# Chunk 1's second projection as seven products of quarters, four more blocks transposed by DMA, and new order tables

## The chip, the core and the metric

The kernel runs on one core of a Trainium2 chip. The metric is the device time of one execution in microseconds (us), the median over runs. The engines are named as in the profile: PE (TensorE matmul), PEld (its weight loads), DVE (VectorE), ACT (ScalarE), POOL (GpSimd), SP (SyncE, which here only issues DMAs).

## The reference, cut to what matters

A linear attention with decay over 64-token blocks gives an array x of 3072 tokens by 512; two projections with a sine between them follow.

```python
def _attn_ref(q, k, v, lam):            # (4, 8, 768, 64) each, lam (8,)
    ...
    for b in range(nb):
        ...
        intra = np.einsum('bhic,bhjc->bhij', qb, kb) * Dmask[None]
        intra = np.einsum('bhij,bhjd->bhid', intra, vb)
        inter = np.einsum('bhid,bhde->bhie', qb * lam_pow[None], kv_state)
        out[:, :, sl] = intra + inter
        kv_state = lam_block[None, :, None, None] * kv_state + np.einsum('bhsd,bhse->bhde', kb_dec, vb)

def _moe_ref(x, w_in, w_out, alpha):    # (3072, 512), (512, 2048), (2048, 512), (2048,)
    h = x @ w_in
    s = np.sin(alpha * h)
    g = h + s * s / (alpha + 1e-09)
    return (g @ w_out).astype(np.float32)
```

## The kernel before, in words

**Blocks and chunks.** The attention is done in 24 blocks of 128 tokens, 6 for each of the 4 batches. Four blocks make a chunk of 512 tokens, and there are 6 chunks, 0 to 5. Chunk 0 is blocks 0 to 3, and so on. While PE works on the projections of one chunk, the attention of later blocks is put between its matmuls.

**Attention of a block.** `load_q` and `load_kv` bring q, k and v as float32 through SP's queue (rings of six blocks). `scale_block` writes them as bfloat16: q and k are multiplied by powers of lam (`L462`, `L472`, `L480`, `L492`), v is only copied (`L486`, `L495`). Then q and k have to be transposed into `qkT`. For blocks under `TD` = 12 PE does it (`piece_Q` for q of two blocks, `L534`; `piece_T` for k of one, `L511`; `piece_K` in the first blocks), and DVE or ACT copy the result out of PSUM (`L516`, `L543`). For blocks from `TD` on SP issues one DMA that transposes both (`L501`). `piece_G(s, t)` is the rest on PE: the scores of block s (`L612`), whose product with the mask is DVE's `Sm` (`L623`), and the output (`L694`, `L707`, `L716`) and the state (`L656`) of block t. The output goes to `xT` (`L726`), the state to `Zd` or `Zc` (`L666`, `L672`).

**First projection.** `unit_A` (`L822`, four matmuls of 512 columns) or `unit_A2` (`L856`, eight of 256) makes one 128-row slice of h, or two halves of slices, in one PSUM bank. ACT takes the sine (`L832`, `L866`), ACT or POOL squares it (`L836`/`L837`, `L870`/`L871`), DVE adds (`L839`, `L874`) and writes `gT`. Three banks take turns.

**Second projection, plain.** In chunks under `SC` = 2, that is 0 and 1, `unit_B` adds up 16 slices for 128 tokens in four steps of four matmuls of 512 columns (`L887`): 64 matmuls for a chunk. ACT copies each of the four results (`L901`) and a DMA stores it.

**Second projection by seven products.** From chunk `SC` on the product of `gT` and `w2` is cut into quarters, and seven products of quarters take the place of eight. `weight_sums` (`L930`) makes five sums or differences of quarters of `w2`, three in buffers of their own and two in place over `w2`; `token_sums` (`L953`) makes five of `gT` for each chunk, in four parts each, 20 instructions for a chunk. `unit_P` (`L975`) is one product for 128 tokens, eight matmuls of 256 columns; 14 of them make a chunk. `finish` takes each result out of PSUM: products 3 and 1 by a copy (`L1012`), the others by an add or a subtraction on DVE (`L1015`, `L1021`).

**Order.** The program first lists its steps with what each reads and writes, and numbers them. Tables written out by hand in `_Plan.ORDER` say for PE, ACT, DVE, POOL and SP in which order the engine takes the steps; where a step is allowed on several engines, the table in which it stands decides. Every engine works through its list strictly in order, and semaphore waits are derived from reads and writes. A pair such as `(42,112)` in PE's table is filler: 42 matmuls of 112 columns on a constant tile (`L1134`), whose result nobody reads.

**Beside it.** `weight_sums(True)` stands ahead of chunk 2's units and `weight_sums(False)`, the two in place, ahead of chunk 3's. A key "select" in reads and writes keeps POOL's `affine_select` steps at the start apart.

Of the kernel before, what the change touches and what calls it, by code (L numbers as in the profile page):

```python
# [13 lines left out]
class _Op:  # L14


    def __init__(self, eng, emit, dur, reads, writes, dma, after, issue, lat, runs=64):
# [13 lines left out]
        self.knows = None  # L31


class _Plan:
# [17 lines left out]
        ),  # L52
        "ACT": (
# [16 lines left out]
        ),  # L70
        "DVE": (
# [30 lines left out]
        ),  # L102
    }

# [104 lines left out]
def bass_lightning_attn__then__act_snake_kernel(  # L209
# [15 lines left out]
    NB = S // BL  # L225
# [1020 lines left out]
```

## Time and profile before

| What | Value |
|---|---|
| Times of three runs | 210.68, 211.11, 211.37 us; median 211.11 us |
| Profiled execution | span 209.8 us from the first to the last instruction; the page gives no other time for it |
| Busy share of the span | PE 97%, PEld 64%, DVE 76%, ACT 76%, POOL 60% |
| Granted TensorE clock | 1.000 of full speed, mean over the span |
| HBM read, written | 27.28 MB, 6.29 MB |
| Chain that ended last, by engine | PE 83%, DVE 6%, DMA 3%, SP's queue 3%, ACT 2% |

The three runs lie 0.9 to 1.6 us above the span of the profiled execution: an execution's time also holds what lies around its first and last instruction. A busy share is an average over the whole span. A matmul's end is modelled in the trace, so what PE needs for a group is better read from the chain of waits, which gives a group's time on the path, than from the durations of its matmuls. Rows of the view of groups give busy time and the mean of one instruction, then the idle time of the engine ahead of it.

### The profile page before, as it was taken

The numbers are of one execution on the slowest core, as the hardware profiler recorded it, in microseconds if no ns is written. First come the engines' busy times: TensorE is split into PE (matmuls) and PEld (weight loads), VectorE is DVE, ScalarE is ACT, GpSimd is POOL, SyncE is SP. The second block draws the span as 40 slices with busy tenths as digits, with TensorE's granted clock in tenths as the row PEclk, the third lists the DMA queues.
The fourth block names the chain that finished last, engine by engine and source line by source line (L and its number), as shares of the span: only waits on it lengthen the run. The fifth ranks groups of instructions, "written<-read, shape, count | busy, mean of one in ns | idle before, by whom it ended". The sixth has DMA issues, their size and how long they took to land.

```text
span 209.8 us, 4867 instructions
## 1 busy us (share of the span) xinstructions
PE 203.5 (97%) x1975; PEld 134.3 (64%) x1975; DVE 160.3 (76%) x266; ACT 158.7 (76%) x294; POOL 126.9 (60%) x130
## 2 busy tenths in 40 slices
PE   7979999999999999999998999999999999999995
PEld 6847444457677776555555667766667765666894
DVE  4884557563999866868899799889698699777643
ACT  4949995968998989999997887787963889568210
POOL 7075354994469578679885392944581957378300
DMA  4999999999998999999999920190000004000514
GB/s 141 310 318 232 206 213 237 246 229 256 220 264 205 227 245 230 223 233 196 246 271 228 213 53 0 33 271 2 3 0 3 0 23 179 3 0 0 200 40 163
DMA packets 78998, 33.35 MB, mean 159 GB/s; under 512 B 55408, under 2 KB 76160, under 8 KB 78976
## 3 DMA queue, kind: packets, MB, share of 16 engines
q1 hardware_dynamic: 73744, 27.14, 56.2%
q0 software_dynamic: 3696, 3.67, 10.5%
q10 hardware_dynamic: 1536, 2.24, 3.3%
q8 instruction: 15, 0.25, 0.5%
q14 instruction: 7, 0.06, 0.1%
HBM read 27.28 MB, written 6.29 MB: 160 GB/s over the span
## 4 chain that ended last, share of the span: by engine, by line
PE 83%; DVE 6%; DMA 3%; SPq 3%; ACT 2%; issue 1%
PE bank L822 27%; PE bank L975 22%; PE bank L887 13%; PE bank L856 10%; DMA v<-in_v_dram 3%; PE bank L716 3%; SPq L315 3%; PE bank L612 3%; DVE gT L839 2%; PE bank L694 1%; DVE Sm L623 1%; PE bank L511 1%; PE bank L656 1%; DVE w L930 1%; PE bank L534 1%; PE bank L707 1%
## 5 line engine op out<-in xcount | busy, mean ns | idle before, releaser
L822 PE MATMUL bank<-xT,w 128*128 128x512 bf16 x296 | 70.5, 379 | 0.0
L839 DVE SCALAR_TENSOR_TENSOR gT<-u,rinv,bank 128x512 bf16<-128x512 bf16 x74 | 53.6, 742 | 18.2 <-ACT u L836 12.5
L832 ACT ACTIVATE t<-bank,alpha 128x512 bf16<-128x512 f32 x74 | 50.0, 684 | 21.0 <-PE bank L822 20.5
L822 PEld LDWEIGHTS bank<-xT,w 128*128 128x128 bf16 x296 | 28.3, 98 | 28.4 <-DVE gT L839 0.4
L836 ACT ACTIVATE u<-t 128x512 bf16<-128x512 bf16 x59 | 36.5, 628 | 1.3
L837 POOL TENSOR_TENSOR u<-t 128x512 bf16<-128x512 bf16 x15 | 16.0, 1066 | 34.1 <-ACT t L832 30.5
L953 POOL TENSOR_TENSOR gT<-gT 128x512 bf16<-128x512 bf16 x24 | 27.8, 1172 | 11.2 <-DVE Xs L953 6.0
L623 DVE TENSOR_TENSOR Sm<-bank,mask 128x1024 bf16<-128x1024 f32 x24 | 29.1, 1218 | 4.3 <-PE bank L648 1.8
L887 PE MATMUL bank<-w,gT 128*128 128x512 bf16 x128 | 31.4, 380 | 0.0
L874 DVE SCALAR_TENSOR_TENSOR gT<-u,rinv,bank 128x256 bf16<-128x256 bf16 x44 | 18.8, 476 | 7.8 <-ACT u L870 6.1
L472 POOL TENSOR_TENSOR qk<-q,Lq 128x512 bf16<-128x512 f32 x20 | 21.2, 1075 | 2.8 <-DMA q<-in_q_dram 2.8
L856 PE MATMUL bank<-xT,w 128*128 128x256 bf16 x176 | 22.2, 273 | 0.0
L492 POOL TENSOR_TENSOR qk<-k,Lk 128x512 bf16<-128x512 f32 x20 | 20.9, 1053 | 0.6 <-DMA k<-in_k_dram 0.6
L866 ACT ACTIVATE t<-bank,alpha 128x256 bf16<-128x256 f32 x44 | 18.9, 476 | 2.0 <-PE bank L856 1.5
L887 PEld LDWEIGHTS bank<-w,gT 128*128 128x128 bf16 x128 | 11.7, 98 | 12.2
L856 PEld LDWEIGHTS bank<-xT,w 128*128 128x128 bf16 x176 | 16.4, 98 | 3.5 <-issue 0.3
L953 POOL TENSOR_TENSOR Xs<-gT 128x512 bf16<-128x512 bf16 x13 | 16.1, 1235 | 1.5 <-DVE gT L839 1.4
L975 PE MATMUL bank<-w,gT 128*128 128x256 bf16 (+1 forms) x136 | 16.3, 266 | 0.0
L975 PE MATMUL bank<-w,Xs 128*128 128x256 bf16 (+1 forms) x136 | 16.0, 267 | 0.1
L975 PE MATMUL bank<-ws,gT 128*128 128x256 bf16 x128 | 15.8, 273 | 0.0
L975 PEld LDWEIGHTS bank<-w,gT 128*128 128x128 bf16 x136 | 12.6, 98 | 3.2
L975 PEld LDWEIGHTS bank<-w,Xs 128*128 128x128 bf16 x136 | 12.4, 98 | 2.8 <-DVE osb L1021 0.3
(101 smaller groups left out, 276.0 us busy)
## 6 DMA issues: line engine op xcount, KB each, us to landing
q<-in_q_dram SPq DMA_DIRECT2D x12, 512.0 KB, 6.2
k<-in_k_dram SPq DMA_DIRECT2D x24, 256.0 KB, 5.5
v<-in_v_dram SPq DMA_DIRECT2D x24, 256.0 KB, 5.4
out_dram<-osb SPq DMA_DIRECT2D x14, 256.0 KB, 2.5
w<-in_moe_w_out_dram POOLq DMA_DIRECT2D x4, 512.0 KB, 11.4
w<-in_moe_w_in_dram POOLq DMA_DIRECT2D x3, 512.0 KB, 9.0
ws<-in_moe_w_in_dram SPq DMA_DIRECT2D x2, 512.0 KB, 7.5
out_dram<-osb ACTq DMA_DIRECT2D x8, 128.0 KB, 4.0
```

What stands on the lines that cost most here:

```text
L472: lambda e, a=a: e.tensor_tensor(qk2[:, j:j + 2, 4 * a:4 * a + 4, :], q32[:, jq, 4 * a:4 * a + 4, :, :].rearrange("p h t d -> p t h d"), b ...
L492: lambda e: e.tensor_tensor(qk2[:, j, H:2 * H, :], block32(k32, jl), lk, ALU.mult), 1.05,
L623: op("DVE", lambda e: e.tensor_tensor(Sm[js][:, :, :], banks[:, 512 * b0:512 * b0 + 1024].rearrange("p (c i) -> p c i", i=128), bass.AP(ma ...
L822: ins = e.matmul(ps[hb][:, c0:c1], w1[:, kc, 128 * m:128 * (m + 1)], xT[x][:, kc, c0:c1], start=(kc == 0 and c0 == lo), stop=(kc == NKC - ...
L832: op("ACT", lambda e: e.activation(t16[ju][:, w], ps[hb][:, w], ACTF.Sin, scale=alpha[:, m:m + 1]), 0.69 if hi - lo == TCH else 0.475, [ba ...
L836: lambda e: (e.activation(u16[ju][:, w], t16[ju][:, w], ACTF.Square) if e is nc.scalar else e.tensor_tensor(u16[ju][:, w], t16[ju][:, w], ...
L839: op("DVE", lambda e: e.scalar_tensor_tensor(out=gT[g][:, m, w], in0=u16[ju][:, w], scalar=rinv[:, m:m + 1], in1=ps[hb][:, w], op0=ALU.mul ...
L856: ins = e.matmul(ps[hb][:, 256 * i:256 * i + 256], w1[:, kc, 128 * (m + i):128 * (m + i + 1)], xT[x][:, kc, lo:lo + 256], start=(kc == 0 a ...
L866: op("ACT", lambda e, i=i: e.activation(t16[ju][:, 256 * i:256 * i + 256], ps[hb][:, 256 * i:256 * i + 256], ACTF.Sin, scale=alpha[:, m + ...
L887: ins = e.matmul(ps[ob][:, w], gT[g][:, m, 128 * s4:128 * (s4 + 1)], w2[:, m, w], start=(m == 0), stop=(m == NM - 1),)
L953: e.tensor_tensor(dst, in0, in1, alu), 0, rd, wr))
L975: ins = e.matmul(ps[ob][:, lo + d0:lo + d1], lhs, rhs[:, d0:d1], start=first and p == 0, stop=(p == NM // 2 - 1), skip_group_check=True)
```

## The change

It does six things at once.

1. `SC` becomes 1. Chunk 1's second projection is done by seven products: 14 `unit_P` in place of 16 steps of `unit_B`, with 20 `token_sums` instructions more. Both calls of `weight_sums` move ahead of the second halves of chunk 1's first projection. From chunk 2 on `piece_G` takes its output bank from the three banks of the first projection (before from chunk 3 on).
2. `TD` becomes 8. Blocks 8 to 11 are transposed by DMA. Their `piece_Q` (two) and `piece_T` (four) on PE go, and with them the copies out of PSUM. What followed from `TD` before as the first block of a loop follows from a new constant, `LB` = 12.
3. Most copies and scalings may stand on several engines: `AD` is ACT or DVE, `DP` is DVE or POOL, `ADP` all three.
4. "select" goes. Where a POOL step is marked `some` (four of the `affine_select`), it and its neighbours on POOL wait for one another through a semaphore.
5. Four activations at the start (`Lq4`, `Lp`, `Lk`, `Lq`) also read `warm`, so they stand behind the table load of the exponential.
6. All five order tables are new.

What the new tables say, counted step by step (before, then after):

| Kind of step | before | after |
|---|---|---|
| copies of v | ACT 20, POOL 4 | ACT 4, POOL 15, DVE 5 |
| scalings of q and k | DVE 7, POOL 41 | DVE 15, POOL 33 |
| `token_sums` | DVE 43, POOL 37 | DVE 50, POOL 50 |
| `weight_sums` | DVE 7, POOL 3 | DVE 5, POOL 5 |
| results of products out of PSUM | DVE 28, ACT 10 | DVE 38, ACT 7 |
| results of `unit_B` out of PSUM | ACT 8 | ACT 2, DVE 2 |
| copies of transposes out of PSUM | DVE 9, ACT 11 | DVE 6, ACT 8 |
| DMA transposes on SP | 12 | 16 |

From the second halves of chunk 1's first projection on, PE's table has the products of chunk 1 between chunk 2's units where the steps of `unit_B` stood. SP's table has the loads up to q of block 10, then the transposes of blocks 8 and 9, then v of 8 and 9, the transposes of 10 and 11, v of 10; before, v of blocks 8 and 9 stood ahead of q of block 10. POOL's table has, from q of block 4 to the last scaling that the transpose of block 8 reads: two q of block 4, a square, k of 4, a weight sum, v of 4, a weight sum, one q of 6, a weight sum, k of 7, k of 8, a square, two q of 8. At the start the fillers are (15,128), (15,512), then (12,128) and (7,128); before they were 102 in 10 groups, the first (42,112) and (30,128). ACT issues its DMA for alpha behind the first logarithm, not ahead of it, and `Lq4` is the last of the four exponentials, not the first. Two of the four first scalings of q and two of the four of k are POOL's; before one of eight was.

The diff, with the tables left out:

```diff
+        self.some = False
+        self.strict = None
...
-        if d.eng != o.eng or d.dma is not None:
+        if d.eng != o.eng or d.dma is not None or d is o.strict:
...
+        last = None
+        for o in order:
+            if o.eng == "POOL" and o.dma is None:
+                if last is not None and (o.some or last.some):
+                    o.strict = last
+                    o.deps.add(last)
+                last = o
...
-    TD = 12
+    TD = 8
+    LB = 12
...
-    SC = 2
-    QD = ((0, 0), (0, 2), (1, 0), (1, 2))
+    SC = 1
+    AD = (("ACT", 0, 0), ("DVE", 0, 0))
+    DP = (("DVE", 0, 0), ("POOL", 0, 0))
+    ADP = (("ACT", 0, 0), ("DVE", 0, 0), ("POOL", 0, 0))
...
-                   ported(op(QE(a, t),
+                   ported(op(DP,
...
-                ported(op((("ACT", 0.62, 0.0), ("POOL", 1.05, 0.3)) if s > 11 else "ACT",
+                ported(op(ADP,
...
-                op("ACT", lambda e: e.copy(osb[jo][:, w], ps[ob][:, w]), 0.59, [bank(ob)], parts)
+                op(AD, lambda e: (e.copy if e is nc.scalar else e.tensor_copy)(osb[jo][:, w], ps[ob][:, w]), 0.59, [bank(ob)], parts)
...
             pieces = pieces_of(8, None, False) + pieces_of(10, 9, False)
+            if SC == 1:
+                weight_sums(True)
+                weight_sums(False)
             for i in range(8):
                 unit_A2(1, 2 * i, 1, (5, 6, 4)[(i + 2) % 3])
+                if SC == 1 and i % 2:
+                    token_sums(1, i // 2)
...
-            block = TD
+            block = LB
...
-                if c == SC + 1:
+                if c == SC + 1 and SC > 1:
                     weight_sums(False)
```

More of the change, by code (lines that the diff above doesn't have):

```diff
@@ L382, in cast_w1_first @@
                 for lo in (0, 256):
-                    op("DVE",
+                    op(AD,
                        lambda e, lo=lo: (e.copy if e is nc.scalar else e.tensor_copy)(
@@ L446, in _ @@
             op("ACT", lambda e: e.copy(alpha[:, :], ps[4][:, 0:NM]), 0.2, [bank(4), "warm"], ["alpha"])
-            def QE(s, a):
-                return "DVE" if (s, a) in QD else "POOL"
             def ported(o):
@@ L478, in scale_block @@
                     for a in range(2) if s % 2 == 0 else ():
-                        eng, dur = ("DVE", 0.68) if s + a < 3 else ("POOL", 1.05)
-                        ported(op(eng, lambda e, a=a: e.tensor_tensor(
+                        ported(op(DP, lambda e, a=a: e.tensor_tensor(
                             qk2[:, j:j + 2, H + 4 * a:H + 4 * a + 4, :],
@@ L483, in scale_block @@
                             bass.AP(Lp, n * H + 4 * a, [[NP * H, 128], [H, 2], [1, 4], [0, D]]), ALU.mult),
-                           dur, [("k32", jl + a), "Lp"], [("k2", j, a), ("k2", j + 1, a)]))
+                           0.68, [("k32", jl + a), "Lp"], [("k2", j, a), ("k2", j + 1, a)]))
                     for a in range(2) if s % 2 == 0 else ():
-                        ported(op("ACT" if s and not a else "POOL", lambda e, a=a: (e.copy if e is nc.scalar else e.tensor_copy)(
+                        ported(op(ADP, lambda e, a=a: (e.copy if e is nc.scalar else e.tensor_copy)(
                             v2[:, j:j + 2, 4 * a:4 * a + 4, :],
@@ L538, in piece_Q @@
                     if len(tbs) == 2:
-                        op("ACT", lambda e, a=a: e.copy(qkT[:, jt:jt + 2, 2 * a:2 * a + 2, :], tps[a]),
+                        op(AD, lambda e, a=a: (e.copy if e is nc.scalar else e.tensor_copy)(
+                            qkT[:, jt:jt + 2, 2 * a:2 * a + 2, :], tps[a]),
                            0.59, [bank(tbs[a])], [("qT", jt, a), ("qT", jt + 1, a)])
@@ L569, in piece_K @@
                 for t in range(2):
-                    op("ACT" if s else (("DVE", 0.43, 0.0), ("ACT", 0.6, 0.0)),
+                    op(AD,
                        lambda e, t=t: (e.copy if e is nc.scalar else e.tensor_copy)(qkT[:, jt + t, 4:8, :], tps[t]),
@@ L665, in then @@
                         r = slice(64 * h, 64 * h + 64)
-                        op("ACT" if s < NP else (("ACT", 0.36, 0.0), ("DVE", 0.43, 0.0)), lambda e, r=r: (e.copy if e is nc.scalar else e.tensor_copy)(
+                        op(AD, lambda e, r=r: (e.copy if e is nc.scalar else e.tensor_copy)(
                             Zd[s % 2][r, :, r], ps[ZB][r, :].rearrange("p (a b) -> p a b", b=128)[:, :, r] if s < NB else
@@ L737, in evict @@
                 P.lead = -20
[L738 to L739 removed]
+                for a0, a1 in ((0, 2), (2, 4)) if len(obs) > 1 else ((0, 4),):
+                    op(AD, lambda e, a0=a0, a1=a1: (e.copy if e is nc.scalar else e.tensor_copy)(
                         xT[c % RX][:, a0:a1, BL * i4:BL * (i4 + 1)].rearrange("p a (u x t) -> p a u t x", u=nq // 2, t=2),
                         ps[obs[a0 // 2 % len(obs)]][:, 128 * a0:128 * a1].rearrange(
[L742 removed]
+                            "p (a u t x) -> p a u t x", a=a1 - a0, u=nq // 2, t=2)), 0.4,
                        [bank(obs[a0 // 2 % len(obs)])], [("xT", c % RX, i4, a) for a in range(a0, a1)])
@@ L1011, in finish @@
                 if i in (1, 3):
-                    op("ACT", lambda e: e.copy(c1 if i == 1 else ny, got), 0.59 if n == 2 else 0.37, [bank(ob)], kc if i == 1 else kn)
+                    op(AD, lambda e: (e.copy if e is nc.scalar else e.tensor_copy)(c1 if i == 1 else ny, got), 0.59, [bank(ob)], kc if i == 1 else kn)
                     return
@@ L1199, in _ @@
                             prep(block + 2)
-                        piece_G(block if block < NBLK else None, block - 1 if block > TD else None,
+                        piece_G(block if block < NBLK else None, block - 1 if block > LB else None,
                                 3 - 3 * (done // 4 % 2) if c <= SC else other())
```

28 lines of the change are left out of this document (12 added, 16 removed), and 111 rows, old and new, of the table ORDER.

## The prediction

> **What bounds the kernel now.** I read the page first, then the chain of waits, then busy time by stretches.
>
> ```profile
> span 209.8 us, 4867 instructions
> PE 203.5 (97%) x1975; PEld 134.3 (64%) x1975; DVE 160.3 (76%) x266; ACT 158.7 (76%) x294; POOL 126.9 (60%) x130
> PE 83%; DVE 6%; DMA 3%; SPq 3%; ACT 2%; issue 1%
> ```
>
> PE is on the path for 83% of the span. The chain of waits (start us, length us, what), some of its pieces:
>
> ```profile
> 7.63 6.83 DMA v<-in_v_dram
> ...
> 19.16 0.87 PE bank L856 x8
> ...
> 32.08 3.45 PE bank L887 x16
> ...
> 59.38 0.49 PE bank L534 x8
> ...
> 62.71 0.33 PE bank L612 x8
> ...
> 64.02 0.22 PE bank L511 x4
> ...
> 65.10 0.33 PE bank L612 x8
> ...
> 130.45 2.62 PE bank L975 x24
> ```
>
> Up to 19 us the chain runs through the loads of the first blocks and their attention. From the first projection at 19.16 us on it is PE's queue nearly to the end. So the time is a beginning of 19 us, PE's work, PE's waits, and an end of 2 to 3 us. Busy time by stretches shows where PE waits (PE, PEld, DVE, ACT, POOL, then clock, DMA share, GB/s):
>
> ```profile
> 49.00:103.00 54.00, 54.00 (x580) 35.37 (x579) 43.37 (x79) 49.61 (x102) 38.99 (x37) 1.00 1.07 229
> 100.00:110.00 10.00, 10.00 (x75) 5.29 (x73) 9.47 (x12) 9.45 (x18) 8.72 (x8) 1.00 1.20 266
> 110.00:120.00 10.00, 9.44 (x84) 6.00 (x82) 8.19 (x13) 8.18 (x14) 4.43 (x5) 1.00 1.09 227
> 120.00:130.00 10.00, 9.89 (x98) 6.43 (x97) 10.00 (x16) 7.53 (x14) 6.95 (x7) 1.00 0.19 35
> ```
>
> From 49 to 103 us PE never goes idle, with DVE busy 80% of the time. From 100 to 130 us DVE is busy 27.66 of 30 us, and PE loses 0.56 + 0.11 = 0.67 us. That is the price of a nearly full DVE in this kernel, and the number I lean on most below.
>
> **The change part by part: PE's work.** Chunk 1's second projection loses 64 matmuls of L887, at 3.45 / 16 = 0.216 us each, 13.80 us, and gains 14 x 8 = 112 matmuls of L975, at 2.62 / 24 = 0.109 us, 12.23 us: 1.57 us less. The transposes of blocks 8 to 11 leave PE: two for q at 0.49 and four for k at 0.22, 1.86 us less. PE's work falls by 3.43 us, and since PE is on the path all through these stages, so does the time, if nothing else fills the gap.
>
> **DVE.** The costs of the steps that are added or move (busy, mean ns of one):
>
> ```profile
> L953 DVE TENSOR_TENSOR Xs<-gT 128x512 bf16<-128x512 bf16 x19 | 12.3, 658 | 0.1
> L953 DVE TENSOR_TENSOR gT<-gT 128x512 bf16<-128x512 bf16 x24 | 12.2, 532 | 0.1
> L480 DVE TENSOR_TENSOR qk<-k,Lp 128x512 bf16<-128x512 f32 x3 | 2.0, 689 | 0.0
> L1021 DVE TENSOR_TENSOR osb<-bank,kept 128x512 f32<-128x512 f32 x6 | 4.1, 684 | 0.5 <-PE bank L975 0.5
> L543 DVE COPY qkT<-bank 128x1024 bf16<-128x1024 bf16 x3 | 2.1, 692 | 0.4 <-PE bank L534 0.4
> L516 DVE COPY qkT<-bank 128x512 bf16<-128x512 bf16 x5 | 2.1, 424 | 2.3 <-PE bank L511 2.3
> ```
>
> I compare the old and new DVE tables between the first unit of chunk 1 and the end of chunk 2's units, 49 to 103 us before. Leaving aside a unit or two that cross the border, new there are 9 token sums (0.59 each, 5.3 us), 3 scalings (0.69, 2.1), 2 copies of v, 5 results of products (0.684, 3.4) and one result of `unit_B`. Gone are 5 copies of transposes (two at 0.69, three at 0.42, 2.7 us), a weight sum and a state copy (taken as 0.69 and 0.42). No row shows DVE copying v; by L480, which reads as much float32 and multiplies, it is at most 0.69, and by L516, a copy of as many bfloat16, at least 0.42: I take 0.55, 1.1 us. The result of `unit_B` I take as L1021, 0.7. The sum is 12.6 - 3.8 = 8.8 us more, so 43.4 becomes 52.2 us of DVE beside 54 - 3.4 = 50.6 us of PE: full, about level with PE, since the busy time of instructions in a run also overlaps a little, which the means do not show. The rows from 100 to 130 us say what that costs: 0.67 us in 30 us, so 1.2 us in 54. The lowest is nothing, if the order hides it; the highest is the rival below. I take 1.2.
>
> ACT hands over 16 copies of v and gains little; it is not near the path there. Waits such as `Sm`'s sit on DVE behind token sums now, and PE's three first-projection banks wait for DVE's additions in turn; `piece_G` in chunk 2 takes one of those three banks more, as it already does from chunk 3 on. That is within the 1.2. The wait of 0.67 itself I leave where it is: chunk 3's stage gains about as much work on DVE as chunk 2's.
>
> **SP's queue and the transposes.** Transposes as issued (duration on the queue, then to landing), the loads of v, and POOL's work ahead of them:
>
> ```profile
> L501 SPq DMA_TRANSPOSE qkT<-qk x12: 1239/1782/2932, 72.9 to 136.3; - x12
> DMA to landing us min/median/max: 3.1/4.6/6.7
> v<-in_v_dram SPq DMA_DIRECT2D x24, 256.0 KB, 5.4
> L472 POOL TENSOR_TENSOR qk<-q,Lq 128x512 bf16<-128x512 f32 x20 | 21.2, 1075 | 2.8 <-DMA q<-in_q_dram 2.8
> L930 POOL TENSOR_TENSOR ws<-w 128x1024 bf16<-128x1024 bf16 x2 | 4.3, 2128 | 0.0
> L837 POOL TENSOR_TENSOR u<-t 128x512 bf16<-128x512 bf16 x15 | 16.0, 1066 | 34.1 <-ACT t L832 30.5 <-DVE gT L874 3.6
> 36.24 2.04 POOL L472 TENSOR_TENSOR qk<-q,Lq 128x512 bf16<-128x512 f32 x2 [0.67 <-DMA q<-in_q_dram]
> ```
>
> POOL's first scaling of block 4 starts at 36.24, on a landing that the change doesn't move. From there to the last input of block 8's transpose its new table has 8 scalings of q and k and a copy of v (9 at 1.08 at most, 9.7), 3 weight sums (6.4) and 2 squares (2.1): 18.2 us, so the transpose is issued at about 54.4 and lands at 59.0, at worst 61.1. Block 8's scores stood at 62.71 before; in the new order they have one more unit ahead (0.87) and lose the q and k transposes (0.71), so still about 62.9. The transpose is hidden by 2 to 4 us. But v of block 8 now waits in SP's queue behind the transposes of 8 and 9, the second of which is issued when POOL has done one more square and one more k (56.6) and takes 1.8: v starts at about 58.4 and lands at 63.8 by the median, and POOL's copy ends past 64.3. Its reader is the output in the piece that stood at 65.10; with one unit between the two pieces it now comes at 62.9 + 0.33 + 0.87 = 64.1, and the output 0.33 later. I put 0.3 us on this wait; if v lands early it is 0.
>
> **The beginning.** `Lq4` comes a little later, POOL takes three more of the eight first scalings at 1.08 us instead of DVE's 0.69, and POOL's last copy of v stands behind a memset and a DMA issue. The last loads of v, 6.83 us from issue to landing, still decide, which hides most of it: 0.3 us, between 0 (all of it hidden; the loads themselves are issued no earlier, so there is no gain) and 3 x 0.39 = 1.2. The end is the same work, about 0.
>
> **Sum.** 209.8 - 1.57 - 1.86 + 1.2 + 0.3 + 0.3 = 208.2 us of span, 1.6 less. The runs' median, 211.11, stands 1.3 us above the span: 209.5 us.
>
> **A shared port: row, then rule.** Token sums on DVE collide with POOL:
>
> ```profile
> L953 DVE TENSOR_TENSOR Xs<-gT x19: 407/419/1359, 92.1 to 196.2; 128x512 bf16<-128x512 bf16 x19
> 107.05 1.16 POOL L953 TENSOR_TENSOR gT<-gT 128x512 bf16<-128x512 bf16 x1
> 107.22 1.27 DVE L953 TENSOR_TENSOR Xs<-gT 128x512 bf16<-128x512 bf16 x1
> ```
>
> The same instruction takes 0.42 us, or 1.27 when it starts inside one of POOL's and ends just after it. The means 0.53 and 0.66 hold this as often as it happened at POOL's 60%. The Trainium skill (GPSIMD Engine Reference, Specifications) says that POOL shares its SBUF interfaces with VectorE, and that VectorE instructions with two SBUF inputs contend. The trace agrees, with 1.27 against 0.42 us. By that rule the scalings that move to DVE would contend as well, which no row here shows.
>
> **The rivals.**
>
> *DVE becomes the bound (slower).* Against my sum speaks that POOL takes some 17 us more over the whole run (13 token sums at 1.16, 15.1; two weight sums, 4.3; 11 copies of v at half a scaling or more, 5.9; less 8 scalings, 8.6), so that in the stage from 49 to 103 us a token sum on DVE nearly always meets a busy POOL. The 14 token sums there at up to 1.27 instead of 0.59, and the 3 scalings and 2 copies of v held up by half a POOL step (0.5), add up to 9.5 + 2.5 = 12 us; half of it is 6. DVE then needs 55 to 58 us beside 50.6 of PE, and the loss is 4.5 to 7 in place of 1.2: 213 to 215. It decides from the point at which the mean token sum passes 0.8 us. For it: DVE would be level with PE already. Against it: from 100 to 130 us DVE was as full, with POOL at 8.72 of 10 for a third of it, and PE lost 0.67. Chance 0.23.
>
> *The order hides all of it.* No loss on DVE, and the old 0.67 goes too: 207.6 to 208.3. Chance 0.10.
>
> *PE's clock falls at the start.* The fillers, before:
>
> ```profile
> 1.52 3.55 PE L1134 MATMUL bank<-Xs 128*128 128x112 bf16 x42 [1.52 <-DVE Xs L410]
> 5.16 1.85 PE L1134 MATMUL bank<-Xs 128*128 128x128 bf16 x30
> ```
>
> 42 of 112 columns take 3.55 us, 0.75 ns a column; 30 of 128 columns at 5.16 us take 0.48. So PE begins slow and is fast by 5 us. The new table has few fillers between 8 and 14 us, where PE has little else. If PE went slow again, chunk 0's first units would cost what the fillers did, 1.3 us more: 210.8, no change that a measurement tells. The Trainium skill (TensorE: Matmul & The Clock Gate, HAM oscillation) has the clock halved after an idle window of about 3.4 us; the trace before, granted clock 1.00 in each stretch shown, has no such gap to test it. Chance 0.08.
>
> *The transposes come late,* SP's queue standing behind a POOL that is slower than summed. One that had lost its cover of 2 to 4 us and landed at the maximum would cost 6.7 - 4.6 = 2.1 us: 211.6, or more with a second one. Chance 0.07.
>
> **How the numbers follow.** My forecast, 208.3 to 210.4, has 0.52. About 0.3%, 0.6 us, is what a measurement of this kernel can tell from no change: 210.5 to 211.7 is "same". Faster: 0.49 of the forecast's chance and 0.10 of the second rival, 0.59. Same: 0.03 of the forecast, 0.03 of DVE's, 0.05 of the clock's, 0.02 of the late transposes', 0.13. Slower: the other 0.28. Range 207.4 to 213.2: it takes in the full gain and DVE's rival at its lower price. The forecast's own range is 208.3 to 210.4.
>
> **What would show it.** Right: 64 fewer matmuls of L887 and 112 more of the 256-column product, no L534 or L511 after block 7, four more transposes; DVE over 90% busy from about 49 to 100 us with PE idle there for 0.5 to 2 us; token sums on DVE with a mean under 0.7 us. Wrong: stretches of the chain on DVE longer than 3 us in chunk 2's stage, PE waiting for `qkT` or v of blocks 8 to 11, or a first unit later than 20 us.

## The result, and the profile after

The changed kernel takes 223.23 us (median of four runs, 222.14 to 224.01) against 211.17 us (210.68 to 211.37) for the kernel before, run beside it: 1.057 times as long, interval 1.053 to 1.061. It is 5.7% slower, 12 us, where 1.6 us less had been forecast. 223.2 lies outside the range given (207.4 to 213.2) and on the other side.

The page of the changed kernel, in the lines that answer to those of before: span, busy shares, PE's busy tenths and granted clock in 40 slices, the chain by engine.

```profile
span 221.6 us, 4803 instructions
PE 202.2 (91%) x1916; PEld 134.0 (60%) x1938; DVE 185.5 (84%) x291; ACT 146.7 (66%) x268; POOL 151.8 (68%) x148
PE   7679999997989997878999999999898999799995
PEclk9999999999999999996999999999999999999999
PE 42%; DVE 36%; POOL 7%; ACT 7%; DMA 4%; issue 3%; DVEq 0%; ACTq 0%
```

PE carried 83% of the chain before and carries 42% now; DVE went from 6% to 36%. DVE is busy for 25 us more, POOL for 25 us more (160.3 and 126.9 before). One slice shows a clock of 0.6.

Where the time was lost is read by stages, with borders at the first unit of chunk 1 (49.5 us before, 52.0 after) and the first unit of chunk 3 (107.3 and 116.0). Their work is the same but for the change itself and one product of chunk 2 (0.87 us of PE), which by the order tables is done ahead of the second border after, and behind it before. Before, then after (length, then PE, PEld, DVE, ACT, POOL busy, clock, DMA share, GB/s):

```profile
20.00:49.50 29.50, 29.50 (x197) 14.85 (x197) 17.82 (x27) 23.21 (x42) 18.58 (x17) 1.00 1.17 229
49.50:107.30 57.80, 57.80 (x617) 37.25 (x615) 46.63 (x83) 53.57 (x108) 41.89 (x41) 1.00 1.08 230
107.30:209.80 102.50, 99.20 (x861) 68.69 (x859) 82.47 (x135) 68.02 (x115) 55.82 (x49) 1.00 0.30 81
```

```profile
20.00:52.00 32.00, 30.56 (x200) 15.00 (x203) 23.60 (x32) 21.78 (x40) 20.92 (x18) 1.00 1.15 223
52.00:116.00 64.00, 57.76 (x632) 41.26 (x637) 61.12 (x100) 49.22 (x98) 47.74 (x44) 0.97 0.85 180
116.00:221.60 105.60, 98.41 (x841) 67.09 (x850) 88.44 (x139) 64.67 (x108) 68.12 (x60) 1.00 0.40 104
```

The three stages are longer by 2.5, 6.2 and 3.1 us, 11.8 in all. In the middle one DVE is busy for 61.1 of 64.0 us and PE stands still for 6.2, where before it had no idle time at all. What PE waits for (us in total, times, longest), before in the first fence, the longest five after in the second; a wait of 1.5 us ahead of the first filler, the same in both, is left out:

```profile
PE bank L648 <- POOL v L486: 0.9, 1, 0.9
PE bank L694 <- DVE gT L839: 0.6, 1, 0.6
```

```profile
PE bank L984 <- DVE gT L962: 2.8, 2, 2.0
PE bank L831 <- DVE gT L848: 2.0, 3, 1.1
PE bank L456 <- DMA alphaT<-in_moe_alpha_dram: 1.8, 1, 1.8
PE bank L831 <- DVE gT L883: 1.3, 2, 1.1
PE bank L542 <- DVE xT L735: 1.0, 1, 1.0
```

(The change moves line numbers by some nine: `L953` is now `L962`, `L975` `L984`, `L822` `L831`.) All but one of these are DVE's. The same instructions have also become longer. Groups on DVE after (busy, mean ns of one, idle time ahead), the token sums first:

```profile
L962 DVE TENSOR_TENSOR gT<-gT 128x512 bf16<-128x512 bf16 x28 | 20.0, 730 | 0.7 <-PE bank L984 0.6
L962 DVE TENSOR_TENSOR Xs<-gT 128x512 bf16<-128x512 bf16 x22 | 16.7, 767 | 0.0
L481 DVE TENSOR_TENSOR qk<-q,Lq 128x512 bf16<-128x512 f32 x7 | 8.4, 1194 | 0.0
L500 DVE TENSOR_TENSOR qk<-k,Lk 128x512 bf16<-128x512 f32 x4 | 3.9, 972 | 0.0
L503 DVE CAST v<-v 128x512 bf16<-128x512 f32 x5 | 2.7, 534 | 0.0
```

The token sums had means of 532 and 658 ns before. Of the scalings I had taken 0.69 us; they take 0.97 and 1.19. And pieces of the chain (start, length, what), three from just ahead of the middle stage and two from its worst place:

```profile
45.63 1.64 DVE Ta L939
48.41 2.39 DVE qk L481
50.80 0.64 DVE xT L735
...
95.97 0.50 DVE v L503
96.47 3.78 DVE gT L962 x3
```

At 50.80 `xT` stands behind a scaling of 2.39 us, and PE's transposes wait for it. At 96.47 three token sums take 3.78 us, and the third product of chunk 1 waits for the last of them. That wait has a price of its own (PE and clock columns as above):

```profile
98.00:100.00 2.00, 0.31 (x1) 0.00 (x0) 2.00 (x2) 1.61 (x3) 2.00 (x3) 1.00 1.34 227
100.00:101.00 1.00, 0.70 (x7) 0.61 (x8) 1.00 (x3) 0.08 (x1) 1.00 (x2) 0.96 1.34 227
101.00:104.00 3.00, 3.00 (x24) 2.18 (x21) 2.97 (x5) 0.00 (x0) 1.97 (x2) 0.50 0.26 82
104.00:105.00 1.00, 1.00 (x24) 0.64 (x21) 0.16 (x1) 0.16 (x1) 0.00 (x0) 0.83 0.08 16
```

PE stood still from about 98.3 to 100.3 us. Some 0.6 us after it had started again, its granted clock fell to 0.50, and stayed there for 3.4 us (0.08 us of the second row, all of the third, 0.34 of the fourth, as the means give it). At half speed 3.4 us lose about 1.7. It does not happen each time: of the four runs three have a mean clock of 0.992 and take 223.17 to 224.01 us, and one has 1.000 and takes 222.14.

### The profile page after: what moved, and what is told of

It is laid out like the page before. It is cut to its first block, busy times and chain, and to the rows that moved or that the text cites. A ratio compares the mean times of both kernels' runs of the same rounds, so it can differ in the third digit from the quotient of the medians.

```text
span 221.6 us, 4803 instructions
## 1 busy us (share of the span) xinstructions
PE 202.2 (91%) x1916; PEld 134.0 (60%) x1938; DVE 185.5 (84%) x291; ACT 146.7 (66%) x268; POOL 151.8 (68%) x148
## 3 DMA queue, kind: packets, MB, share of 16 engines
q10 hardware_dynamic: 960, 1.19, 1.9%
## 4 chain that ended last, share of the span: by engine, by line
PE 42%; DVE 36%; POOL 7%; ACT 7%; DMA 4%; issue 3%; DVEq 0%; ACTq 0%
PE bank L984 16%; PE bank L831 14%; DVE gT L848 7%; DVE gT L962 5%; DVE Sm L632 5%; DVE gT L883 4%; DVE Xs L962 4%; POOL gT L962 3%; ACT t L841 3%; DMA alphaT<-in_moe_alpha_dram 2%; PE bank L896 2%; PE bank L865 2%; POOL u L846 2%; DVE qk L481 2%; PE bank L621 2%
## 5 line engine op out<-in xcount | busy, mean ns | idle before, releaser
L831 PE MATMUL bank<-xT,w 128*128 128x512 bf16 x279 | 68.4, 380 | 5.1 <-DVE gT L848 2.0
L848 DVE SCALAR_TENSOR_TENSOR gT<-u,rinv,bank 128x512 bf16<-128x512 bf16 x74 | 53.7, 742 | 18.8 <-ACT u L845 14.3
L962 POOL TENSOR_TENSOR gT<-gT 128x512 bf16<-128x512 bf16 x32 | 38.8, 1220 | 13.5 <-DVE Xs L962 12.3
L831 PEld LDWEIGHTS bank<-xT,w 128*128 128x128 bf16 x296 | 27.3, 98 | 32.7 <-DVE gT L848 5.5
L962 POOL TENSOR_TENSOR Xs<-gT 128x512 bf16<-128x512 bf16 x18 | 22.6, 1255 | 9.7 <-DVE gT L848 9.7
L984 PE MATMUL bank<-w,gT 128*128 128x256 bf16 (+1 forms) x168 | 20.9, 277 | 3.4 <-DVE gT L962 2.8
L984 PEld LDWEIGHTS bank<-w,gT 128*128 128x128 bf16 x168 | 15.9, 101 | 8.6 <-DVE gT L962 3.5
L962 DVE TENSOR_TENSOR gT<-gT 128x512 bf16<-128x512 bf16 x28 | 20.0, 730 | 0.7 <-PE bank L984 0.6
L984 PE MATMUL bank<-ws,gT 128*128 128x256 bf16 x160 | 20.3, 273 | 0.0
L984 PE MATMUL bank<-w,Xs 128*128 128x256 bf16 (+1 forms) x168 | 19.6, 268 | 0.0
L984 PEld LDWEIGHTS bank<-ws,gT 128*128 128x128 bf16 x160 | 15.5, 98 | 4.5
L984 PEld LDWEIGHTS bank<-w,Xs 128*128 128x128 bf16 x168 | 15.5, 98 | 3.3
L962 DVE TENSOR_TENSOR Xs<-gT 128x512 bf16<-128x512 bf16 x22 | 16.7, 767 | 0.0
```

The costliest lines, as they stand in the source:

```text
L831: ins = e.matmul(ps[hb][:, c0:c1], w1[:, kc, 128 * m:128 * (m + 1)], xT[x][:, kc, c0:c1], start=(kc == 0 and c0 == lo), stop=(kc == NKC - ...
L848: op("DVE", lambda e: e.scalar_tensor_tensor(out=gT[g][:, m, w], in0=u16[ju][:, w], scalar=rinv[:, m:m + 1], in1=ps[hb][:, w], op0=ALU.mul ...
L962: e.tensor_tensor(dst, in0, in1, alu), 0, rd, wr))
L984: ins = e.matmul(ps[ob][:, lo + d0:lo + d1], lhs, rhs[:, d0:d1], start=first and p == 0, stop=(p == NM // 2 - 1), skip_group_check=True)
```

## The experiments

Theory: DVE became the bound, by more work and by steps that wait for POOL at a shared port. Rivals: the new order by itself; the DMA transposes; the beginning.

**Token sums taken out.** In three kernels token sums of chunk 1 only clear their target: those on DVE, those on POOL, and all 20. Waits and tables stay; a clear takes 0.27 us on DVE and 0.52 on POOL.

```diff
-  e.tensor_tensor(dst, in0, in1, alu)
+  e.memset(dst, 0.0) if c == 1 and e is nc.vector else e.tensor_tensor(dst, in0, in1, alu)
   # second kernel: e is nc.gpsimd; third: c == 1 alone
```

> The changed kernel with one thing left out: the 13 token sums of chunk 1 that stand on DVE only clear their target (their values are missing from the output); all waits and the order stay. In the changed kernel these 13 took 11.9 us of DVE between 73 and 104 us. Theory (DVE is the bound of this stage, by its work and by the port it shares with POOL): DVE gets about 10 us back where PE waits for it, and the time falls by 5 to 9 us, to 214 to 218; the clock's dip at 100 to 110 us goes with PE's gap before it. Rival (the beginning, the transposes by DMA or the new order set the time): under 1 us less, 222 to 224.

> The changed kernel with one thing left out: the 7 token sums of chunk 1 that stand on POOL only clear their target (their values are missing from the output); DVE's list of steps is untouched. Theory with the port: DVE's steps with two operands in SBUF lose part of their 12.2 us of lengthening between 40 and 105 us because POOL is busy for 6 to 8 us less, and the time falls by 2 to 5 us. Theory without the port (DVE simply has too many steps): DVE does the same work as before, the time falls by less than 1 us, and token sums on DVE keep their mean of 0.75 us. Rival (beginning, transposes, order): no difference.

> The changed kernel with all 20 token sums of chunk 1, on DVE and POOL, only clearing their targets (their values are missing from the output). Alone, DVE's 13 were worth 5.1 us and POOL's 7 2.95. If the prices add: 215 to 216; if each side's price was the other's waiting at the port: 216 to 218. What then remains above 211 belongs to the beginning and to the stages of chunks 3 to 5, whose steps are those of before.

Measured: without DVE's 13 218.16 us (5.1 less; 1.034 of before, 1.031 to 1.036), without POOL's 7 220.28 (3.0 less; 1.044, 1.039 to 1.049), without all 20 217.15 (6.1 less; 1.029, 1.026 to 1.032). The second is the telling one, by its durations: not a step of DVE was changed, and DVE's token sums became shorter by themselves (the kernel without POOL's sums; 730 and 767 ns in the changed kernel):

```profile
L963 DVE TENSOR_TENSOR gT<-gT 128x512 bf16<-128x512 bf16 x28 | 18.4, 675 | 0.7 <-PE bank L985 0.6
L963 DVE TENSOR_TENSOR Xs<-gT 128x512 bf16<-128x512 bf16 x22 | 15.7, 722 | 0.0
```

All three run at a clock of 1.00: without the sums PE's gap at 98 us is gone, and the half clock with it. So some 1.7 us of each price is the clock's, and against the one run of the changed kernel without the dip (222.14) the three save 4.0, 1.9 and 5.0 us. That the first prices do not add (5.1 + 3.0 against 6.1) says nothing of the port, since the dip is counted twice in the sum; counted once, 6.4 is close to 6.1. In the stage of chunk 2 DVE has 29.50 us of work in 32.10 without the sums, and had 36.55 in 38.60:

```profile
77.60:109.70 32.10, 31.77 (x321) 22.23 (x325) 29.50 (x54) 25.76 (x48) 22.52 (x25) 1.00 0.97 203
```

```profile
77.40:116.00 38.60, 33.89 (x321) 23.01 (x325) 36.55 (x54) 25.95 (x49) 28.96 (x27) 0.96 0.81 172
```

But 6 us of the loss remain.

**DVE's moved scalings and copies taken out too (`cut_more`).** Besides the 20 sums, the 7 scalings of q, 4 of k and 5 copies of v that DVE has from block 4 on only clear their target.

```diff
-  lambda e: e.tensor_tensor(qk2[:, j, H:2 * H, :], block32(k32, jl), lk, ALU.mult)
+  lambda e: e.memset(qk2[:, j, H:2 * H, :], 0.0) if e is nc.vector else e.tensor_tensor(...)
   # and so for q and v
```

> The changed kernel with all 20 token sums of chunk 1 cut as before and, besides, DVE's 7 scalings of q, 4 of k and 5 copies of v from block 4 on (15.0 us of DVE) only clearing their targets (these values are missing from the output too); POOL keeps its steps. It asks what the 6 us are that remained without the sums (217.15 against 211). Theory (the rest too is DVE, held up at the port in its scalings): 211 to 214. Rival (the beginning, the transposes by DMA, ACT, or the order of steps that don't use the port): 216 to 217.5.

212.99 us, 4.2 less again: 1.010 of before (1.008 to 1.012). So 10.2 of the 12 us go, clock included, with steps that the change put on DVE, and with seven that it put on POOL. This kernel does less than either of the two: the 11 scalings and 5 copies stand on no engine at all, and before, POOL and ACT had them. It shows that the loss hangs on these steps where they stand, not that it comes from their having moved. What PE still waits for is mostly later `gT` (2.5 us behind 40 us) and the beginning.

**The same steps put back on POOL and ACT (`scal_back`).** Everything complete; only the engines of these steps change.

```diff
   # order tables: 7 q and 4 k scalings from DVE's table to POOL's,
   # copies of v from POOL's (11) and DVE's (5) to ACT's, each at its place in time
```

> The changed kernel, complete, with the engines of one group of steps put back: from block 4 on all scalings of q and k on POOL (11 leave DVE) and all 16 copies of v on ACT (11 leave POOL, 5 leave DVE); every step stays at its place in time. DVE had these 16 for 8.4 + 3.9 + 2.7 = 15.0 us; POOL gains about 11 x 1.08 - 11 x 0.70 = 4 us. Theory (DVE and the port): 4 to 8 us faster than the changed kernel, 215 to 219, with less lengthening of the token sums that remain on DVE. Rival (the added token sums alone are too much for DVE, whatever the scalings do): under 2 us faster. Rival (POOL becomes the bound): slower than 223, PE waiting for POOL's squares and scalings.

222.33 us, ratio 1.053 (1.050 to 1.056) where the changed kernel has 1.057 (1.053 to 1.061): no difference that can be told; the theory had 215 to 219. DVE gets rid of 15.0 us of steps, and its busy time falls by 9.8 us, from 185.5 to 175.7. Its token sums take back 1.8 us in all (38.5 us for 36.7): the first group is longer now, the second shorter (842 and 706 ns, 730 and 767 in the changed kernel).

```profile
L962 DVE TENSOR_TENSOR gT<-gT 128x512 bf16<-128x512 bf16 x28 | 23.1, 842 | 0.7 <-PE bank L984 0.6
L962 DVE TENSOR_TENSOR Xs<-gT 128x512 bf16<-128x512 bf16 x22 | 15.4, 706 | 0.0
```

So 9.8 us less of DVE bought nothing by themselves, and this speaks against DVE's sum of work as the whole cause. On the chain POOL has 18% where it had 7, ACT 15% where it had 7, and PE's longest wait in total is still for a sum on DVE (`gT` of `L848`, 4.2 us in 8 waits). Why the time stayed was not tried further.

**The port by itself.** A kernel of its own: eight instructions of each kind on DVE, alone and beside a stream on POOL.

```diff
+  for stream in (None, token sums, copies of v):        # on POOL, 14 of them
+      for kind in (token sum, scaling, copy of v, bfloat16 copy, bank sum):   # on DVE, 8 of them
```

> A kernel that computes nothing of the reference: eight each of a token sum (128x512 bfloat16, two operands in SBUF), a scaling (float32 operand and a broadcast column, bfloat16 result), a copy of v (float32 to bfloat16), a copy in bfloat16 and a sum of a bank with SBUF on DVE, first alone, then beside 14 token sums on POOL, then beside 14 copies of v on POOL. Theory (a shared port): alone 0.42 and 0.69 us for the first two; beside POOL's token sums both wait for the end of a POOL step, 0.8 to 1.3 us or more, and POOL's steps lengthen from about 1.05 to over 1.2 us; the bank sum keeps its time, the copies too or nearly. Rival (memory bandwidth): all five kinds lengthen by a like share, well under a factor of two. Beside POOL's copies of v the theory has the same lengthening if they hold the port, none if only two-operand steps of POOL do.

Groups by stretch of time: a token sum alone; a token sum, a scaling, a bfloat16 copy and a bank sum, each beside POOL's token sums; a token sum beside POOL's copies of v.

```profile
L34 DVE TENSOR_TENSOR xb<-ab 128x512 bf16<-128x512 bf16 x8 | 2.8, 419 | 0.0
```

```profile
L34 POOL TENSOR_TENSOR yb<-bb 128x512 bf16<-128x512 bf16 x9 | 11.5, 1306 | 0.0
L34 DVE TENSOR_TENSOR xb<-ab 128x512 bf16<-128x512 bf16 x8 | 10.3, 1354 | 1.4 <-POOL yb L34 1.4
```

```profile
L37 DVE TENSOR_TENSOR xb<-ff,L 128x512 bf16<-128x512 f32 x8 | 12.4, 1618 | 6.8 <-POOL yb L34 6.8
```

```profile
L43 DVE COPY xb<-ab 128x512 bf16<-128x512 bf16 x8 | 9.2, 1220 | 6.8 <-POOL yb L34 6.8
```

```profile
L34 POOL TENSOR_TENSOR yb<-bb 128x512 bf16<-128x512 bf16 x6 | 6.7, 1158 | 0.0
L46 DVE TENSOR_TENSOR gf<-bank,z 128x512 f32<-128x512 f32 x8 | 4.9, 682 | 6.8 <-POOL yb L34 6.8
```

```profile
L34 DVE TENSOR_TENSOR xb<-ab 128x512 bf16<-128x512 bf16 x8 | 5.9, 808 | 10.2 <-POOL yb L40 10.2
```

The two engines take turns: DVE does one step for each of POOL's. A token sum goes from 419 to 1354 ns, a scaling from 686 to 1618, and POOL's own sum from 1158 to 1306 or 1543. A copy with its source in SBUF waits too, which I had expected of no copy: 285 ns alone, 1220 beside POOL. A sum that reads a bank is untouched (682), and so is POOL beside it. Beside POOL's shorter copies of v a token sum takes 808. It is a lock, not a sharing of bandwidth: token sum, scaling and bfloat16 copy all wait for about the same time, 0.93 to 0.94 us, which is POOL's token sum alone (1.16) less about 0.2. This agrees with the Trainium skill (SBUF — State Buffer, Who interferes with whom), by which the port pair of DVE and POOL is held exclusively and the loser blocks, and casts and copies may take it as well as instructions with two SBUF inputs.

**Old and new tables mixed.** Four complete kernels: the new steps with the old engines and order for all else; the reverse; the seven products alone with the old order; and the new kernel with the old engines and order from chunk 3 on. Tables were merged by the times at which each step ran.

```diff
 # new steps, old order: SC = 1, TD = 8     # old steps, new order: SC = 2, TD = 12
 # products alone, old order: SC = 1, TD = 12     # old order from chunk 3 on: SC = 1, TD = 8
```

> The new steps (seven products and sums of chunk 1, transposes of blocks 8 to 11 by DMA), complete, with every step that both kernels have on the engine and at the place that it had before; the new steps, and the weight sums, stand on the engines of the changed kernel at the corresponding places. Theory (the new work on DVE and POOL is the cause): 216 to 221, with chunk 2's stage several us longer than 30.7 us and the later stages as before. Rival (the new engines of common steps and their new order are the cause): 209 to 212.

> The other half: the steps of before (chunk 1's second projection by 64 matmuls of 512 columns, transposes of blocks 8 to 11 on PE), complete, with the engines and the order of the changed kernel for every common step. Theory: 212 to 215, since the added sums are gone from DVE and POOL. Rival (the new engines and order): 217 to 222.

> As the new steps on the old engines and order, but with the transposes of blocks 8 to 11 on PE as before: chunk 1's products alone. Theory (the sums): 217 to 222, no faster than with the DMA transposes. Rival (the transposes by DMA come late and cost more than their 1.86 us of PE): 2 us or more faster than with them.

> The changed kernel, complete, but every step that stood behind 107 us before has the engine and the place in the order that it had before. From the first unit of chunk 3 to the end PE took 100.6 us before and 103.8 in the changed kernel, with the same steps. If the later engines and order are a loss of their own: 219.5 to 221, 3 us faster than the changed kernel. If the later loss is the wake of chunk 2's stage: within 0.7 us of 223.2.

250.94, 249.16, 241.81 and 246.69 us. All four fall outside what any theory gave, and they tell nothing of either cause: at the seams of a merged table PE waits in single places far longer than anywhere in the changed kernel (2.0 us), for example 7.9 us for one transpose in the first and 6.8 us for one weight sum in the last, and the clock falls behind such gaps (mean 0.93 to 0.97). What they do show is how much these tables carry: a step a few places too early blocks all that stands behind it.

**Another order for the same steps.** So the order had to be tested with tables that are fitted to the steps. A model of the five queues was built from the traces' durations with the lock of the port in it, and a search over it gave new tables. First for the whole kernel, with the kernel before as control:

```diff
 # ORDER: order searched anew, same steps, same engines (after_order);
 # engines searched too: the changed steps, before + TD = 8, before
```

> The changed kernel, complete: the same steps on the same engines, only the order inside the tables is new. It was searched for with a small model of the five queues, made from the traces' own durations and landings, in which a step of DVE or POOL with all its operands in SBUF holds one port (as the run of the port alone showed). The model gives 222 us for the changed kernel's table (traced 221.6), 206 for the table of before (traced 209.8), 204 without the port for both, and 203 for the new table. Theory now (the steps collide at the port and block those queued behind them, because the table puts them together; the amount of work would fit): 205 to 213. Rival (the amount of work on DVE and POOL is too much in any order): 217 to 223.

> The changed kernel's steps, complete, with engines as well as order searched anew by the same model (146 of some 700 steps change their engine, 49 of them token sums, 32 scalings or copies of v). Theory: 202 to 211, some 3 us under the kernel with order alone. Rival (amount): 215 or more.

> The kernel before with only the transposes of blocks 8 to 11 by DMA, complete, engines and order searched anew by the same model (201 us). If the prediction's term of 1.86 us of PE is real: 1 to 2.5 us under the kernel before with its order searched anew. If late landings eat it: equal or slower.

> The control: the kernel before, complete, its steps unchanged, engines and order searched anew by the same model (202 us). What it gains is the search's gain alone: theory 207 to 211 (before: 211.1). If its time falls as far as the others', the new products and transposes are worth nothing of their own.

225.03, 227.74, 227.59 and 221.01 us. The control itself lost 10 us, all of it ahead of chunk 1's first unit (59.7 us for 49.5), where the landings of loads decide and the model had them wrong. The first kernel (`after_order`) lost 6 us there (58.0 us for 52.0 in the changed kernel), so its total tells little; but from that unit to the end it takes 165.2 us, with two steps of `unit_B` more left to do, the changed kernel 169.6 and the kernel before 160.3. With the same steps on the same engines, the order alone is worth 4.4 us there. Its three stretches from chunk 1's first unit on (borders at the first units of chunks 2 and 3):

```profile
58.00:86.40 28.40, 26.71 (x337) 20.24 (x336) 25.63 (x46) 24.05 (x52) 23.69 (x21) 1.00 1.07 223
86.40:119.00 32.60, 30.76 (x314) 20.60 (x308) 31.54 (x52) 25.10 (x47) 23.68 (x22) 1.00 1.01 192
119.00:223.20 104.20, 99.30 (x861) 68.41 (x860) 81.71 (x138) 64.43 (x109) 63.75 (x59) 1.00 0.29 80
```

Of the 4.4 us the dip of the clock, which is missing here, is about 1.7. The search was repeated with the tables kept up to 45 us:

> The changed kernel, complete: same steps, same engines; the tables are as they are up to 45 us, and from there on the order alone was searched anew with the model of the queues and the port, under landings and durations varied by some per cent (the run with all of the order searched anew lost 10 us ahead of chunk 1, where the model knows the loads badly; from chunk 1's end to its own end it took 137 us, against 142 in the changed kernel and 129 before). Theory (the sums and POOL's steps collide and block the queue because the table puts them together): 209 to 216. Rival (the amount of work on DVE and POOL is too much in any order): 219 to 224.

> The control: the kernel before, complete, its tables kept up to 45 us, order and engines searched anew from there on by the same model. It shows what the search is worth by itself: 207 to 212.

223.75 us (1.059, 1.056 to 1.063) for the changed steps on their engines, and 214.97 (1.020, 1.015 to 1.026) for the control (`before_late`). DVE's token sums did get shorter (571 and 643 ns), and the time did not. But this table has a loss of its own, at its start: PE waits for a scaling on POOL and for `xT`, and its granted clock is 0.50 for 6.8 us from 54.4 us on, which loses about 3.4 us.

```profile
PE bank L542 <- POOL qk L481: 2.9, 1, 2.9
PE bank L865 <- DVE xT L735: 1.6, 1, 1.6
```

From chunk 3's first unit to the end it takes about 101.5 us, some 4 less than the changed kernel (105.6), of which 0.9 is one more product of chunk 2 done earlier. Between two searched tables the new steps remain 8.8 us above the old ones, some 3.4 of it by the clock (the control's engines were free as well). But the control is itself 4 us above the table it started from, and the model was 17 us and more too low for tables of its first search (202 against a span of 219.5 for the control, 201 against 226.3 with the DMA transposes). So these runs do not settle how much of the loss is the amount of work and how much its order: the order is worth several us, and a better one than these may exist.

**The DMA transposes alone.** The kernel before with `TD` = 8; tables searched anew from 45 us on, and then, with all engines as before, from 56 us on (`td8_56`).

```diff
-    TD = 12
+    TD = 8
+    LB = 12          # and ORDER from 45 us (56 us) on
```

> The kernel before with only the transposes of blocks 8 to 11 by DMA, complete, its tables kept up to 45 us and searched anew from there on. If the prediction's 1.86 us of PE is real and the landings are in time: 1 to 2 us under the control. If late landings eat it: equal or slower.

> The kernel before with only the transposes of blocks 8 to 11 by DMA, complete, all engines as before and all tables as before up to 56 us; from there on the order was searched anew with the loads held at their traced times. The run with tables kept to 45 us had lost 6.4 us at 47 to 54 us to a copy of v on ACT that stood ahead of its load, before any of the new transposes; from the first half of chunk 1 to its end it took 142.1 us against 143.9 before. If the 1.86 us of PE are to be had: 209 to 210.5. If the landings of the transposes or POOL's scalings ahead of them eat it: 211 to 214.

217.85 us, 2.9 above its control (and 6.6 above it, 227.59 against 221.01, in the search over the whole table), and 216.22 us (1.026 of before, 1.023 to 1.028), which is above both ranges given. In the first of them a copy of v on ACT stood ahead of its load for 6.4 us, before any new transpose, so it decides little. The last is clean up to the stage in question, and there PE waits for the transposes (waits, then one transpose's piece of the chain):

```profile
PE bank L611 <- DMA qkT<-qk: 4.4, 2, 4.2
```

```profile
62.37 5.92 DMA qkT<-qk
```

The clock is at 0.50 for 3.4 us behind that wait. The transposes of blocks 8 and 9 are issued at 57.7 and 62.4 and land 7.8 and 5.9 us later. In the changed kernel the same ones are issued at 58.4 and 61.4 and land after 3.2 and 3.1 us, with a new order of PE that asks for them later; no PE instruction waits for them. So in none of these three tables were the 1.86 us of PE to be had by moving the transposes alone.

## Why the prediction was wrong, point by point

**The step that failed: DVE's loss of 1.2 us.** The count of its work was near. In the stage from chunk 1's first unit to chunk 3's DVE is busy for 61.1 us where it was for 46.6: 14.5 more. Of that 6.5 is lengthening (durations above the shortest of the same instruction, summed: 8.8 us after, 2.3 before), and 8.0 is left, where 8.8 had been forecast. But I priced a full DVE by the row from 100 to 130 us (0.67 us lost in 30), and the token sums by their old means. Two things were wrong with that. The means belong to a POOL that is 60% busy, and a wait at the port counts as DVE's busy time (a token sum of 0.42 us takes 1.35 beside POOL's). And the row was of a stage in which PE had as much to do as DVE; with DVE ahead of PE its delays reach PE. PE stood still for 6.2 us of that stage, and lost about 1.7 more to the clock. That the stage as a whole is longer by 6.2 too is chance: its work on PE is 2.6 us less (3.43 less one product), so 57.8 - 2.6 + 6.2 + 1.7 = 63.1 of its 64.0 us are found.

**The rival "DVE becomes the bound" came nearest, and its price was too low.** It had the lengthening (half of 12 us; 6.5 measured), the collisions of scalings and copies, and 213 to 215. Its own test, a mean token sum above 0.8 us, is met in the stage (0.93 and 0.90 us for the 13 between 73 and 104 us), not over the whole run (0.73 and 0.77). It counted 17 us more for POOL, and POOL is busy for 25 more. Missing were the stages on both sides, which I put at nothing: PE stood still for 1.4 us between 20 and 52 us (DVE 23.6 us busy for 17.8) and for 7.2 in place of 3.3 from chunk 3 on, where the steps are the same but DVE's list is longer by scalings, copies of v and results of products (88.4 us busy for 82.5). Nor is DVE the only engine there: from 114.6 to 131.0 us the chain runs on POOL, with such pieces as

```profile
116.80 2.67 POOL gT L962 x2
126.55 2.23 POOL gT L962 x2
```

"The old wait stays" and "the end about 0" were not looked at with the port in mind. The row of 1.27 for 0.42 us was quoted, and left out of the sum. That DVE alone is the bound is more than the runs show: `scal_back` took 9.8 us from DVE and gained nothing.

**PE's work, -3.43 us.** The products take what was taken (0.87 us for eight matmuls in the chain), and the transposes of blocks 8 to 11 left PE. Where many of DVE's steps are out of the way, part of it shows: from the first unit of chunk 0 to that of chunk 4, between which both have the same parts, the kernel without the sums and scalings takes 116.9 us (20.0 to 136.9), the kernel before 119.4 (19.0 to 138.4): 2.5 us less. No run shows the whole 3.43, and in the changed kernel waits hide it.

**Transposes and v of block 8: +0.3 us, and the rival of late transposes.** In the changed kernel neither is waited for; the transpose of block 8 is issued at 58.4, not 54.4, and lands at 61.6. The cover held, though the issue came 4 us later than I summed. It does not need DVE: in `scal_back`, with all scalings from block 4 on back on POOL, the transpose of block 8 is issued at 58.6 and lands at 61.7, and PE does not wait for it. What the sum did not see is the landing: in `td8_56` the same transpose is issued earlier, at 57.7, and lands 7.8 us later, at 65.5, above the maximum of 6.7 that I had taken from the trace before.

**The beginning, +0.3 us (0 to 1.2).** The first unit starts at 19.7 in place of 19.0. Not for the reasons given: ACT now issues the load of alpha behind a logarithm that waits for lam, so it lands late and PE's first transposes stand behind it. The chain shows this; no run has that load back in its old place.

```profile
0.81 3.23 DMA lam_bc<-in_lam_dram
...
4.07 5.21 DMA alphaT<-in_moe_alpha_dram
9.28 0.14 issue
9.42 0.20 PE bank L456
```

**The clock.** It did not fall at the start, as that rival had it, but at 101 us, behind PE's wait for DVE.

**What was to show it.** DVE over 90% busy from 49 to 100 us came true (50.1 of 51 us); PE idle for 0.5 to 2 us did not (6.8), nor did token sums under 0.7 us. Of the signs of error, DVE pieces of over 3 us in chunk 2's stage are there (3.78); PE waiting for transposes or v of blocks 8 to 11, and a first unit later than 20 us (19.7), are not.

**What remains.** 10.2 of 12 us go with steps taken out. `cut_more` is still 2.1 us above the kernel before: its beginning is longer by about 1.0, and its stages of chunks 4 and 5 by 3.5 (32.1 us from the first unit of the one to that of the other, 30.1 before; 42.8 from there to the end, 41.3 before), against the 2.5 gained between. This was not tried by itself. And whether a better order would keep the new steps and lose less stays open.

## What to carry to other kernels

A busy share near 100% of the bound's is no plan: price each step that is added to DVE or POOL at what it costs beside the other engine, and add DVE's steps and POOL's steps with all operands in SBUF into one sum, since in the kernel of the port they took turns. Leaving such steps out gave the time back; moving a part of them between DVE, POOL and ACT did not, though DVE was busy for 9.8 us less. With tables in strict order the place of a step counts beside its cost: the same steps on the same engines, in another order, took 4.4 us less behind chunk 1's first unit, and lost it again ahead of it.

## What the runs showed of the hardware

- DVE and POOL took turns one for one where both had all operands in SBUF: a bfloat16 copy of 0.29 us takes 1.22 beside POOL's token sums, a token sum 1.35 for 0.42, a scaling 1.62 for 0.69; POOL's own step goes from 1.16 to 1.31 or 1.54. With one operand of DVE's sum in a bank nothing is lost on either side (0.68 and 1.16).
- One gap of 2.0 us on PE was followed, 0.6 us after its end, by 3.4 us at half clock. The Trainium skill (TensorE: Matmul & The Clock Gate, HAM oscillation) names gaps of over about 3.4 us as what to avoid; here a shorter one was followed by the fall. The length of the gap does not decide alone: one of the four runs of the changed kernel has no fall, and in the profiled run of `before_late` PE waits for 2.6 us in one piece and the clock stays at 1.00.
- The DMA transpose of one block took 3.0 to 4.1 us from issue to landing in the changed kernel (DMA share 0.58 from 58 to 66 us), and up to 7.8 us in `td8_56` (DMA share 1.25 there).
